# Normalizing products that read in order and write with a step of four columns, and two last stores issued whole

## The chip, the core and the metric

The kernel runs on one core of one Trainium2 chip. The metric is the device time of one execution in microseconds (us). Five engines work at the same time, each through its own queue of instructions: TensorE (PE) multiplies matrices, VectorE (DVE) and ScalarE (ACT) do elementwise work, GpSimd (POOL) does casts and issues some DMAs, and SyncE (SP) issues most DMAs. ACT's queue can issue DMAs too. SBUF is the on-chip memory, 128 partitions with one row each; PSUM is the smaller memory that PE writes.

## The reference

Sliding-window attention of 8 batches, 8 heads, 576 positions and 64 channels per head, followed by a two-layer network with a tanh GELU:

```python
B, H, S, D = q.shape                      # 8, 8, 576, 64
scores = (1 / np.sqrt(D)) * np.matmul(q, k.transpose(0, 1, 3, 2))
mask = np.abs(pos[:, None] - pos[None, :]) <= 32
scores = np.where(mask, scores, -1e9)
attn = softmax(scores)                    # over the last axis
x = np.matmul(attn, v).transpose(0, 2, 1, 3).reshape(B * S, H * D)   # 4608 tokens x 512
h = x @ w_in                              # w_in 512 x 2048
g = 0.5 * h * (1 + np.tanh(c * (h + 0.044715 * h ** 3)))
out = g @ w_out                           # w_out 2048 x 512, float32
```

## The kernel before

**Two streams of work on one PE.** The network runs over 9 tiles of 512 tokens (t = 0 to 8). While tile t is multiplied by w_out, the attention of batch b = t + 1 is computed in between: each loop step i issues one product of the network, and the tables PLAN_0, PLAN_1, PLAN_2, PLAN_L and PLAN say after which i a piece of attention is issued (s is a score, m a mask, g or v the sums and weighted values, x the normalizing product). So the order on each engine is written out by hand, and each engine runs its own list in order. Batches 0 and the start of the network are written out one by one ahead of the loop.

**Attention in groups.** A batch has five groups. Groups 0 to 3 are pairs of heads, 64 channels of two heads on the 128 partitions, with the first 480 tokens of the batch (512 in batch 0). Group 4 holds the last 96 tokens (64 in batch 0) of all four pairs. The function score (line 489) multiplies keys and queries on PE; line 502 takes the exponential on ACT; mask (line 511) multiplies by the band on DVE; sum_up (line 516) sums over the keys on PE, and times (line 526) multiplies by the values on PE; invert (lines 553 and 554) takes the logarithm and the exponential of its negative on ACT, which gives one over the sum, in the SBUF tile lt.

**The normalizing product.** The function spread (lines 564 and 571) multiplies the weighted values, which lie in PSUM as float32 (tiles ps_o, ps_od, mm), by lt, float32 in SBUF, on DVE, and writes float16 into xT, the input of the network. Queries are stored four ways interleaved: in PSUM and in lt the columns stand as (j p), j = 0 to 3 outside and p inside, where the token is 4 p + j. In xT the columns stand in the order of the tokens, (p j). So one side of the product has to be walked with a step. In this kernel the two operands are: `x[:, 0:n].rearrange("d (j p) -> d p j", j=4)` takes an element from each of the four rows j in turn, 120 float32 elements (480 bytes) apart in a group of 480, 128 (512 bytes) in batch 0 and 24 or 16 in group 4; the write runs through xT column by column. xT is a ring of 1,536 columns; where a batch crosses its end, line 564 is issued twice, with shorter pieces (192 and 288, or 384 and 96 elements).

**Who uses xT.** ffn_in (line 602) multiplies four chunks of w_in by the four pairs' rows of xT, chunk dc needing pair dc. For the next tile the first three columns n are begun with chunks 0 to 2 (dc = 0, 1, 2 of one column, then of the next) at the end of the loop over i; chunk 3 follows at the head of the next tile. Later tiles compute part of this product with seven half-size products in place of eight (in_product, line 658), for which DVE forms differences of blocks of xT (line 643) and of w_in (in_w, line 632). In w_in16 the columns that belong together are four apart, and in_w reads them through this view:

```python
w_cols = w_in16.rearrange("k d (i p j) -> k d i j p", i=4, j=4)
A11, A12, A21, A22 = (w_cols[:, d:d + 2, c + i, j:j + 2, :] for c in (0, 2) for d in (0, 2))
```

so that line 632 reads float16 elements in SBUF with a step of four columns (8 bytes), runs of 128 elements, and writes float16 without a step.

**The second layer.** ffn_out (line 789) computes gelu(h) by w_out with seven products n = 0 to 6 in place of eight. DVE takes each result out of PSUM (lines 800 to 821: n = 3 is line 812, n = 5 is line 821) and ffn_last (line 830) the last one. Two PSUM banks take turns, and n = 5 adds onto the bank that line 812 has to read first. The masks of the next groups stand on DVE behind such lines.

**Loads of the early batches.** For batch 2 SP issues, in this order, the loads of keys (line 204), two transposing DMAs of queries and keys (lines 435 and 443), which wait for casts on DVE (lines 431 and 441), and then four loads of values (line 416); POOL casts these (line 357), and DVE copies them to the other half of the partitions (pair_v, lines 236 and 237) for times. All DMAs of one queue are issued in the order of its list.

**Stores.** The function store (line 753) splits its rows evenly over the engines named. In the last tile the third quarter (line 823) is stored by SP and ACT in halves of 64 rows, and line 834 stores the last two blocks of 128 rows by 256 columns (block x = 0, then x = 1), each as 64 rows on SP and 64 rows on ACT.

Of the kernel before, what the change touches and what calls it, by code (L numbers as in the profile page):

```python
# [12 lines left out]
ALU = mybir.AluOpType  # L13
# [23 lines left out]
def cut(b):  # L37
    return 120 if b else 128
# [50 lines left out]
def kernel(  # L89
# [9 lines left out]
    nc = tc.nc  # L99
# [3 lines left out]
    NPAIR = H // 2  # L103
# [39 lines left out]
    xT = big.tile([128, NPAIR, RING], FP16, name="xT")  # L143
# [395 lines left out]
    def weigh(b, g, pair=None):  # L539
        pe = groups.pop((b, g))  # L540
        o, d = out_of(pair)
        sum_up(b, g, d, pe)
        times(b, g, o, pe)
        return o, d

    def size(b, g):
        return 4 * cut(b) if g < 4 else 4 * NPAIR * (144 - cut(b))
# [9 lines left out]
    def spread(b, g, o, lt):  # L557
        n = size(b, g)
        if g < 4:
            pos, done, w = b * S % RING, 0, cut(b)  # L560
            by_row = [x[:, 0:n].rearrange("d (j p) -> d p j", j=4) for x in (o, lt)]
            while done < w:
                e = min(w - done, (RING - pos) // 4)
                nc.vector.tensor_tensor(  # L564
                    xT[:, g, pos:pos + 4 * e].rearrange("d (p j) -> d p j", j=4),
                    *(x[:, done:done + e, :] for x in by_row), op=ALU.mult)
                done, pos = done + e, (pos + 4 * e) % RING
        else:
            pos = (b * S + 4 * cut(b)) % RING
            assert pos + n // NPAIR <= RING  # L570
            nc.vector.tensor_tensor(
                xT[:, :, pos:pos + n // NPAIR].rearrange("d r (p j) -> d r p j", j=4),
                *(x[:, 0:n].rearrange("d (r j p) -> d r p j", r=NPAIR, j=4) for x in (o, lt)), op=ALU.mult)


    gTs = {}
# [170 lines left out]
    def store(t, t4, yo, cols=slice(0, 512), *engs):  # L747

        r0 = t * 512 + t4 * 128
        engs = engs or (nc.gpsimd,)  # L750
        rows = 128 // len(engs)
        for i, eng in enumerate(engs):
            eng.dma_start(out[r0 + i * rows:r0 + i * rows + rows, cols], yo[i * rows:i * rows + rows, cols])  # L753
# [71 lines left out]
    def ffn_last(t):  # L825
        py = pys[0].rearrange("p (b c) -> p b c", b=2)
        yo, right = wino["yo"], slice(256, 512)
        for x in range(2):
            part = pys["apart"][:, 0:256] if x and t == NT - 1 else py[:, x, :]
            nc.vector.tensor_tensor(yo[:, x, right], part, yo[:, x, right], op=ALU.add)  # L830
            if t < NT - 1:
                store(t, x, yo[:, x, :])
            else:
                store(t, x, yo[:, x, :], right, nc.sync, nc.scalar)


    cast_open(0)
# [50 lines left out]
    def finish(g, o):  # L888
        times(0, g, o, groups.pop((0, g)))
        spread(0, g, o, lts[g])  # L890
# [80 lines left out]
    for t in range(NT):  # L971
# [58 lines left out]
        for i in range(113 if t else 65):  # L1030
# [9 lines left out]
            for act in plan.get(i, "").split():  # L1040
                kind, at = act[0], int(act[act.index("@") + 1:]) if "@" in act else None
                g = int(act[1:].split("@")[0])
# [16 lines left out]
                elif kind in "np":  # L1059
# [7 lines left out]
                    if kind == "n":  # L1067
                        n = size(1, g)
# [21 lines left out]
                elif kind in "ab":  # L1090
                    if b < B - 1:
                        if kind + str(g) == "a0":
                            cast_open(b + 1)
                        turn_query(b + 1, g) if kind == "a" else turn_keys(b + 1, (g,))
                elif kind == "g":
                    two = []
                    for gg, pair in ((g, at), (g + 1, None)) if g >= 0 else ((2, None), (g, at)):
                        two.append((gg, *group(gg), *out_of(pair), groups.pop(group(gg))))
                    for gg, bb, g1, o, d, pe in two:
                        sum_up(bb, g1, d, pe)  # L1100
                    for gg, bb, g1, o, d, pe in two:
                        times(bb, g1, o, pe)
                    for gg, bb, g1, o, d, pe in two:
                        ods[gg] = (o, invert(bb, g1, d))
                    if g < 0:
                        load_vt(b + 1)
                    if t > 1 and g == 2:
                        load_table(gelu_set)
                elif kind == "v":
                    bb, gg = group(g)  # L1110
                    o, d = weigh(bb, gg, at)
                    ods[g] = (o, invert(bb, gg, d))
                    if t and g < 0 and b + 1 < B:
                        load_vt(b + 1)
                    if t > 1 and g == (3 if att else -1):
                        load_table(gelu_set)
                else:
                    spread(*group(g), *ods[g])
# [16 lines left out]
        if t == 0:  # L1135
            wino_rest(B12)
            load_table(gelu_set)
        else:
            ffn_last(t)
# [31 lines left out]
```

## Time and profile before

| | |
|---|---|
| median of 3 runs | 296.28 us (295.19 to 296.58) |
| the profiled execution | 295.1 us, of which the span from its first to its last instruction is 293.2 us |
| busy: PE, weight loads, DVE, ACT, POOL | 283.9, 196.6, 237.7, 196.8, 66.5 us |
| TensorE clock granted | 0.998 |
| normalizing products | line 564 40 times, line 571 8 times |

A line of groups gives the line of the kernel, the engine, the operation, what it writes and reads, the shape and the count, then the busy time in us, the mean of one in ns, and the idle time of the engine just before them with what ended it. A line of the timeline gives the start in us, the time that the merged run of instructions took, the engine, line, operation and count, and in brackets idle time ahead of it and what ended it. Matmuls overlap: 128x512 ones that follow each other without a wait start 0.216 us apart, though each is shown as 0.38 us long. A queue's own instructions carry a q (SPq, ACTq): for a DMA that is the time that the issue takes, not the transfer.

### The profile page before, as it was taken

The numbers are of one execution on the slowest core, as the hardware profiler recorded it, in microseconds if no ns is written. First come the engines' busy times: TensorE is split into PE (matmuls) and PEld (weight loads), VectorE is DVE, ScalarE is ACT, GpSimd is POOL, SyncE is SP. The second block draws the span as 40 slices with busy tenths as digits, with TensorE's granted clock in tenths as the row PEclk, the third lists the DMA queues.
The fourth block names the chain that finished last, engine by engine and source line by source line (L and its number), as shares of the span: only waits on it lengthen the run. The fifth ranks groups of instructions, "written<-read, shape, count | busy, mean of one in ns | idle before, by whom it ended". The sixth has DMA issues, their size and how long they took to land.

```text
span 293.2 us, 7364 instructions
## 1 busy us (share of the span) xinstructions
PE 283.9 (97%) x2993; PEld 196.6 (67%) x2993; DVE 237.7 (81%) x499; ACT 196.8 (67%) x323; POOL 66.5 (23%) x109
## 2 busy tenths in 40 slices
PE   8889999999999999999999999999999999999994
PEld 3535544557775688668856876688667877887783
DVE  4775377999997988899998899889988987875682
ACT  5865867779477876588558945894679576904800
POOL 4435325102327071105025003500300020011000
PEclk9999999999999999999999999999999999999999
DMA  7999997989999999859998989698810030003014
GB/s 226 274 373 401 353 311 191 252 168 191 263 211 189 242 237 203 241 133 225 131 249 218 182 118 209 179 180 104 244 18 2 2 143 3 0 2 144 0 38 107
DMA packets 112481, 51.00 MB, mean 174 GB/s; under 512 B 96768, under 2 KB 108544, under 8 KB 112192
## 3 DMA queue, kind: packets, MB, share of 16 engines
q1 hardware_dynamic: 89584, 38.81, 59.1%
q0 software_dynamic: 21840, 10.82, 21.3%
q10 hardware_dynamic: 1024, 0.92, 1.1%
q8 instruction: 23, 0.38, 0.6%
q14 instruction: 10, 0.08, 0.1%
HBM read 36.70 MB, written 9.44 MB: 157 GB/s over the span
## 4 chain that ended last, share of the span: by engine, by line
PE 79%; DVE 8%; DMA 6%; SPq 3%; issue 2%; ACT 1%; POOL 1%; ACTq 0%; DVEq 0%
PE mm L789 29%; PE ph L602 15%; PE mm L602 12%; PE pu L658 7%; PE ps_s L489 3%; PE mm L761 2%; DMA wst<-in_moe_w_in_dram 2%; PE py L761 2%; DVE xT L564 2%; SPq L282 2%; DMA vr<-in_v_dram 2%; DVE t L733 2%; DMA qr<-in_q_dram 1%; PE ps_d L516 1%; PE ps_od L516 1%
## 5 line engine op out<-in xcount | busy, mean ns | idle before, releaser
L602 PEld LDWEIGHTS <-w_in 128*128 128x128 f16 x448 | 50.1, 113 | 40.2 <-issue 1.2
L602 PE MATMUL ph<-xT,w_in 128*128 128x512 f16 x240 | 60.2, 379 | 0.3 <-POOL w_in L261 0.3
L602 PE MATMUL mm<-xT,w_in 128*128 128x512 f16 x208 | 53.9, 379 | 0.6 <-DVE xT L564 0.5
L789 PEld LDWEIGHTS <-s 128*128 128x128 f16 x512 | 49.4, 98 | 6.2
L789 PE MATMUL mm<-t,s 128*128 128x256 f16 x376 | 44.9, 273 | 0.0
L789 PEld LDWEIGHTS <-gT 128*128 128x128 f16 x384 | 36.1, 98 | 7.3 <-issue 1.0
L502 ACT ACTIVATE pe<-ps_s 128x960 f16<-128x960 f32 (+1 forms) x31 | 29.5, 975 | 13.7 <-PE ps_s L489 13.6
L753 POOL DMA_DIRECT2D out_dram<-y x28 | 15.2, 548 | 98.9 <-DVE y L821 93.6
L789 PE MATMUL mm<-w_out,gT 128*128 128x256 f16 x256 | 32.6, 273 | 0.0
L610 ACT ACTIVATE gT<-mm 128x512 f16<-128x512 f32 x28 | 16.5, 599 | 22.8 <-PE mm L602 22.5
L743 DVE TENSOR_TENSOR s<-gT 128x512 f16<-128x512 f16 x64 | 26.6, 421 | 5.3 <-ACT gT L610 2.3
L610 ACT ACTIVATE gT<-ph 128x512 f16<-128x512 f32 x38 | 20.9, 607 | 6.8 <-PE ph L602 6.8
L114 ACT ACT_TABLE_LOAD x18 | 23.1, 1283 | 2.2 <-issue 1.9
L554 ACT ACTIVATE lt<-lt 128x480 f32<-128x480 f32 (+3 forms) x36 | 21.1, 585 | 1.2
L511 DVE TENSOR_TENSOR pe<-pe,band 128x960 f16<-128x960 f16 x28 | 18.1, 664 | 0.7 <-ACT pe L502 0.5
L564 DVE TENSOR_TENSOR xT<-ps_od,lt 128x480 f16<-128x480 f32 (+4 forms) x18 | 14.8, 848 | 3.4 <-ACT lt L554 2.2
L526 PEld LDWEIGHTS <-V 128*64 128x64 f16 x520 | 12.6, 112 | 6.5 <-DVE V L237 2.3
L564 DVE TENSOR_TENSOR xT<-ps_o,lt 128x480 f16<-128x480 f32 (+5 forms) x20 | 15.2, 783 | 1.9 <-PE ps_o L526 1.7
L706 ACT ACTIVATE gT<-ph 128x512 f16<-128x512 f32 x22 | 13.2, 601 | 4.8 <-PE ph L602 4.7
L789 PE MATMUL mm<-t,gT 128*128 128x256 f16 x128 | 16.2, 273 | 0.2
L743 DVE TENSOR_TENSOR s<-s,gT 128x512 f16<-128x512 f16 x32 | 14.5, 452 | 1.1
L553 ACT ACTIVATE lt<-ps_od 128x480 f32<-128x480 f32 (+2 forms) x13 | 7.1, 546 | 11.5 <-PE ps_od L526 6.7
(153 smaller groups left out, 484.7 us busy)
## 6 DMA issues: line engine op xcount, KB each, us to landing
kr<-in_k_dram SPq DMA_DIRECT2D x31, 256.0 KB, 8.2
out_dram<-y POOLq DMA_DIRECT2D x28, 256.0 KB, 3.5
qr<-in_q_dram SPq DMA_DIRECT2D x6, 1024.0 KB, 6.1
wst<-in_moe_w_in_dram SPq DMA_DIRECT2D x8, 512.0 KB, 7.8
vr<-in_v_dram SPq DMA_DIRECT2D x12, 256.0 KB, 5.9
wst<-in_moe_w_out_dram SPq DMA_DIRECT2D x2, 1024.0 KB, 10.5
wst<-in_moe_w_out_dram SPq DMA_DIRECT2D x4, 512.0 KB, 7.2
V<-in_v_dram POOLq DMA_DIRECT2D x16, 128.0 KB, 8.7
```

Of the source, the lines that this page charges most:

```text
L114: nc.scalar.add_instruction(mybir.InstLoadActFuncSet(name=nc.get_next_instruction_name(), act_func_set_id=which, ins=[], outs=[]))
L502: nc.scalar.activation(pe, ps[:, :, 0:w], AF.Exp, scale=SCALE)
L511: nc.vector.tensor_tensor(pe, pe, m.rearrange("k (o j) p -> k o j p", o=1).broadcast_to(list(pe.shape)), op=ALU.mult)
L554: nc.scalar.activation(lt[:, 0:n], lt[:, 0:n], AF.Exp, scale=-1.0)
L564: nc.vector.tensor_tensor(xT[:, g, pos:pos + 4 * e].rearrange("d (p j) -> d p j", j=4), *(x[:, done:done + e, :] for x in by_row), op=ALU. ...
L602: nc.tensor.matmul(ph, w_cols[:, dc, fc // 4, fc % 4, :], xT[:, dc, t * 512 % RING:t * 512 % RING + 512], start=(dc == 0), stop=(dc == 3))
L610: nc.scalar.activation(gTs[t][:, fc, :], phs[fc], AF.Gelu_apprx_tanh)
L658: nc.tensor.matmul(ps[:, 256 * h:256 * h + 256], lhs[:, d, h, :], rhs[:, d, :], start=(n in (0, 2, 4) and h == d == 0), stop=(h == d == 1) ...
L706: nc.scalar.activation(gTs[t][:, fc, :], phs[fc], AF.Gelu_apprx_tanh)
L743: nc.vector.tensor_tensor(dst, x, y, op=op)
L753: eng.dma_start(out[r0 + i * rows:r0 + i * rows + rows, cols], yo[i * rows:i * rows + rows, cols])
L789: nc.tensor.matmul(pys["apart"][:, 0:256] if apart else py[:, blk, :], lhsT, wino[w][:, f, :], start=(new and i % (8 if one else 16) == 0) ...
```

## The change

In spread the two operands are now read as they lie (four runs of 120, 128, 96, 48, 72 or 24 elements, or 24 and 16 in group 4), and the write into xT goes along with them, with a step of four columns (8 bytes) from one element to the next. The number of instructions, the elements of each and all waits stay; on DVE line 564 has the form 128x4x120 where it had 128x480. In ffn_last each of the last two blocks is stored whole, 128 rows by 256 columns: block 0 from ACT's queue, block 1 from SP's. SP and ACT issue one DMA each where they issued two; nothing else changes its place on any engine.

```diff
@@ spread
-            by_row = [x[:, 0:n].rearrange("d (j p) -> d p j", j=4) for x in (o, lt)]
+            by_row = [x[:, 0:n].rearrange("d (j p) -> d j p", j=4) for x in (o, lt)]
...
                 nc.vector.tensor_tensor(
-                    xT[:, g, pos:pos + 4 * e].rearrange("d (p j) -> d p j", j=4),
-                    *(x[:, done:done + e, :] for x in by_row), op=ALU.mult)
+                    xT[:, g, pos:pos + 4 * e].rearrange("d (p j) -> d j p", j=4),
+                    *(x[:, :, done:done + e] for x in by_row), op=ALU.mult)
...
             nc.vector.tensor_tensor(
-                xT[:, :, pos:pos + n // NPAIR].rearrange("d r (p j) -> d r p j", j=4),
-                *(x[:, 0:n].rearrange("d (r j p) -> d r p j", r=NPAIR, j=4) for x in (o, lt)), op=ALU.mult)
+                xT[:, :, pos:pos + n // NPAIR].rearrange("d r (p j) -> d r j p", j=4),
+                *(x[:, 0:n].rearrange("d (r j p) -> d r j p", r=NPAIR, j=4) for x in (o, lt)), op=ALU.mult)
@@ ffn_last
-                store(t, x, yo[:, x, :], right, nc.sync, nc.scalar)
+                store(t, x, yo[:, x, :], right, (nc.scalar, nc.sync)[x])
```

## The prediction

> **What bounds the kernel now.** I read the page first, then the chain that ended last, then the groups by form, then the timeline at the places where PE starts late.
>
> ```profile
> PE 283.9 (97%) x2993; PEld 196.6 (67%) x2993; DVE 237.7 (81%) x499; ACT 196.8 (67%) x323; POOL 66.5 (23%) x109
> ...
> PE 79%; DVE 8%; DMA 6%; SPq 3%; issue 2%; ACT 1%; POOL 1%; ACTq 0%; DVEq 0%
> ```
>
> PE is the bound. A shorter DVE instruction is worth only what PE waits for DVE, so the sum has to be made at single places. What the products cost today, and what comparable DVE work costs, by form:
>
> ```profile
> L564 DVE TENSOR_TENSOR xT<-ps_od,lt 128x480 f16<-128x480 f32 x12 | 11.6, 990 | 3.0 <-ACT lt L554 1.8 <-PE ps_od L526 1.2
> ...
> L830 DVE TENSOR_TENSOR y<-mm,y 128x256 f32<-128x256 f32 x15 | 5.7, 419 | 0.9 <-PE mm L789 0.9
> ...
> L821 DVE TENSOR_TENSOR y<-mm,y 128x512 f32<-128x512 f32 x8 | 5.5, 690 | 2.9 <-PE mm L789 2.9
> ...
> L632 DVE TENSOR_TENSOR wcA<-w_in 128x512 f16<-128x512 f16 x2 | 1.4, 696 | 0.0
> ...
> L564 DVE TENSOR_TENSOR xT<-ps_o,lt 128x96 f16<-128x96 f32 x3 | 0.9, 304 | 0.0
> ```
>
> Lines 821 and 830 have the same operands as the product (one in PSUM, one in SBUF, float32) without a step: (690 - 419) / 256 = 1.06 ns per element and 148 ns fixed. The product takes (990 - 304) / 384 = 1.79 ns per element and 132 ns fixed. So reading with a step of 480 bytes costs 0.73 ns more per element.
>
> **Cost of the products after.** Reading in order takes the 0.73 ns away. What the write with a step of 8 bytes adds, no row shows: nothing in the trace writes single elements with a step. The nearest row is line 632, which reads two float16 operands in SBUF with this same step of 8 bytes and takes 696 ns for 512 elements, (696 - 148) / 512 = 1.07 ns per element: no more than a walk without a step. The bounds: at least the unstepped rate, 148 + 480 x 1.06 = 657 ns; at most twice the penalty that the read pays now, 990 + 480 x 0.73 = 1340 ns; between them lies 990, a write that costs what the reads cost. Below 657 nothing is in sight, since the same-shaped rows without any step are not faster. I take 657, by the row with the same step. Saved: 333 ns on each of 20 products of 480, about 360 on the 4 of 512 (1047 to 691), 257 on 11 of 384 (812 to 555), 198 on 4 of 288, 130 on 4 of 192, little on the rest, some 12 of DVE's 237.7 us.
>
> [...]
>
> **Where PE waits for these products.**
>
> ```profile
> 51.80 3.69 DVE L564 TENSOR_TENSOR xT<-ps_od,lt 128x480 f16<-128x480 f32 x4 [1.20 <-PE ps_od L526]
> ...
> 53.24 0.88 PE L602 MATMUL mm<-xT,w_in 128*128 128x512 f16 x2
> ...
> 54.64 0.38 PE L602 MATMUL mm<-xT,w_in 128*128 128x512 f16 x1 [0.51 <-DVE xT L564]
> ...
> 80.25 0.33 PE L516 MATMUL ps_od<-pet,ones 128*64 128x384 f16 x2
> ...
> 80.87 0.42 PE L526 MATMUL ps_o<-pe,V 128*64 128x96 f16 x14 [0.28 <-DVE xT L564]
> ```
>
> First place: the first chunks of tile 1 need pairs 0, 1 and 2 in turn. At the pace of 0.216 us the third matmul would start at 53.24 + 0.43 = 53.67; it starts at 54.64, 0.97 late. The products start 0.92 apart; after, 0.59 apart, so the third ends at 51.80 + 1.18 + 0.66 = 53.64. Gain 0.95.
>
> Second place: two sums of 0.16 us start at 80.25, so the next could start near 80.5; with the base cost of a switch it is 0.35 late, behind four products (two of 384, two of 96: 0.6 us saved). Gain 0.35, if DVE also keeps up with PE's earlier arrival (below).
>
> ```profile
> 171.57 0.70 DVE L812 TENSOR_TENSOR y<-mm,y 128x512 f32<-128x512 f32 x1
> ...
> 172.33 1.03 PE L789 MATMUL mm<-t,gT 128*128 128x256 f16 x8
> ...
> 173.04 0.65 DVE L511 TENSOR_TENSOR pe<-pe,band 128x960 f16<-128x960 f16 x1
> ...
> 173.74 0.39 PE L516 MATMUL ps_d<-pe,ones 128*64 128x480 f16 x2
> ```
>
> Third: line 812 frees the bank that n = 5 adds onto; PE could start at 172.02 (nine matmuls of 0.109 from 171.04), so it is 0.31 late, and the mask behind makes it 0.25 late again at 173.74. Ahead of line 812 stand two split products of 1.06 us each (192 and 288 elements), which lose 0.33 each; 0.66 covers the 0.56. The same place in the next two tiles (202.63 and 232.77, unsplit products) is 0.17 and 0.19 late. Gain 0.9 in all.
>
> The four products of batch 0 (14.3 to 22.1 us) gain nothing: PE at 21.27 waits for POOL's cast of w_in, and that for a DMA that lands at 20.55; the casts hide them. From 84 to 165 and after 235 PE shows no late start beyond 0.2 us that DVE ends: PE's matmuls hide those products.
>
> **What is next late.** The gain at 54 must survive the chain that runs through DVE, SP and the loads of batch 2's values:
>
> ```profile
> 68.94 5.27 DMA vr<-in_v_dram
> 74.21 0.05 issue
> 74.27 0.86 POOL V L357
> 75.12 0.02 issue
> 75.14 0.80 DVE V L236
> 75.94 0.01 issue
> 75.95 0.42 DVE V L237
> ```
>
> PE needs these values from 76.3 us, with no slack. SP issues the loads behind two transposes (63.59 and 64.95) that wait for DVE's casts, and those stand on DVE behind the four products at 51.80, without idle time between. So the casts come 4 x 0.33 = 1.3 us earlier, and SP's transposes and loads with them, into a stretch in which the DMA engines idle (41 to 55 KB per us at 63 to 65 us against 200 to 250 around it). I take it that the values keep up with the 0.95.
>
> **The last stores.** The final product ends at 289.01 + 0.42 = 289.43. SP then still issues block 0's half, and starts block 1's at 289.81; ACT's starts at 290.11 and lands last, 2.0 us on. After, each queue has one issue left: ACT's queue is free at 289.4 and SP's at 289.15, so both start near 289.45. The 128 KB stores at 282.7 land in 1.8 us, the second 0.48 behind the first; two at once would land near 291.3 and 291.8 in place of 292.1. Bounds: 0.6 gained, if both land in 2 us; 0.3 lost, if 256 KB at once queue behind the third quarter's halves. I take 0.25 gained. Nobody waits for them but the end.
>
> **Sum.** 0.95 + 0.35 + 0.9 + 0.25 = 2.45 us. The profiled execution took 295.1 us, 1.9 of it outside the span of 293.2, so it becomes 292.7. It lies 1.2 below the median, at the low end of the three runs; the difference goes onto the median: 296.28 - 2.45 = 293.8. I write 294.0, since the 0.35 needs DVE to keep its lead.
>
> **Rivals.**
> - *Given back at the values.* If the transposes or loads take no earlier slot (SP's own issue of line 435 ends at 62.0 whatever DVE does), PE waits at 76.3 for what it saved at 54. Left: 0.35 + 0.9 + 0.25 = 1.5; 294.8 us. For it: SP's list is in order and the DMA share there is 0.98. Against: the idle DMA stretch.
> - *The step moves, and with it the price.* The write pays what the reads paid; the products stay at 990 ns, and only the stores change: 296.0 us. For it: one stepped stream might cost as much as two. Against: line 632.
> - *Slower: the write is dearer than the reads were.* It decides as soon as a product of 480 takes over 990 ns. At the upper bound, 1340 ns, the third product at 51.8 ends 3 x 0.35 = 1.05 later, and PE with it; at 80.87 DVE is 4 x 0.35 + 0.7 = 2.1 later, less PE's 1.05; line 812 comes 0.7 later in three tiles (2.1) and, with 0.2 of idle time before it, 0.5 later in the two tiles before (1.0). Together 5.2, less 0.25 at the stores: 301.2 us. [...]
>
> **How the numbers follow.** Forecast 0.56, given back 0.14, price moved 0.14, slower 0.16. A difference under 0.5%, 1.48 us, is about what a measurement of this kernel can't tell from none. Of the forecast 0.88 lies beyond that, of the second case half: faster 0.56. Same 0.27: the third case, and what is left of the first two. Slower 0.17. The range goes from 293.0 (all gains, and 0.6 at the stores) to 297.2 (the third case with the runs' spread of 0.6 and a slightly dearer write); it leaves out the dear write. The likeliest case alone spans 293.0 to 294.9.
>
> **What would show it.** Right: line 564 at 480 elements near 657 ns; the matmul of line 602 that starts at 54.64 follows its neighbours at 0.216 us; no late start before line 526 near 80; line 812 ends before PE needs its bank; the values of batch 2 are on DVE about 1 us earlier; two issues fewer at the end. Wrong: a product of 480 at 900 ns or more sinks the sum at once; PE's late start moving from 54 to 76 is the first rival; last landings later than 2.7 us after the last product turn the stores' sign.

## The result and the profile after

The changed kernel is slower: 297.29 us (median) against 295.81 for the kernel before beside it, ratio 1.0062 with a 95% interval of 1.0032 to 1.0091. The ratio is taken over the runs and amounts to about 1.8 us; the two medians lie 1.5 us apart. The forecast was 2.3 us faster. The profiled execution took 296.96 us with a span of 295.3 us (295.10 and 293.2 before).

The busy times of the profile page and the products by form, after:

```profile
PE 284.8 (96%) x2993; PEld 197.1 (67%) x2993; DVE 245.0 (83%) x499; ACT 196.8 (67%) x323; POOL 66.7 (23%) x109
```

```profile
L564 DVE TENSOR_TENSOR xT<-ps_od,lt 128x480 f16<-128x480 f32 x12 | 14.4, 1247 | 2.8 <-ACT lt L554 1.8 <-PE ps_od L526 1.0
...
L564 DVE TENSOR_TENSOR xT<-ps_o,lt 128x96 f16<-128x96 f32 x3 | 1.2, 417 | 0.0
```

A product of 480 takes 1247 ns in place of 990 (657 were forecast), one of 96 takes 417 in place of 304: (1247 - 417) / 384 = 2.16 ns per element, where the stepped read took 1.79. DVE is busy 7.3 us longer. The timeline at the first and the second place of the prediction, and at the bank of line 812:

```profile
51.93 4.46 DVE L564 TENSOR_TENSOR xT<-ps_od,lt 128x480 f16<-128x480 f32 x4 [1.04 <-PE ps_od L526]
...
54.30 0.38 PE L602 MATMUL mm<-xT,w_in 128*128 128x512 f16 x1 [0.54 <-DVE xT L564]
...
55.36 0.38 PE L602 MATMUL mm<-xT,w_in 128*128 128x512 f16 x1 [0.69 <-DVE xT L564]
...
81.91 0.42 PE L526 MATMUL ps_o<-pe,V 128*64 128x96 f16 x14 [0.60 <-DVE xT L564]
...
174.05 1.03 PE L789 MATMUL mm<-t,gT 128*128 128x256 f16 x8 [0.31 <-DVE y L812]
```

PE now waits for the second product and for the third (before, visibly for the third alone), and it waits longer before line 526 at 81.91 and behind line 812 at 174.05. Since PE issues the same 2993 matmuls in the same order, each can be set against its own start before. The delay of PE grew at these matmuls:

| matmul (start before) | waits for | delay added, us |
|---|---|---|
| up to 53.2 us | | 0.13 |
| line 602, 53.75 and 54.64 | the second and third product | 0.59 |
| line 526, 80.87 | the bank that line 564 reads | 0.31 |
| line 526, 136.08 | the bank that line 571 reads | 0.12 |
| line 602, 146.97 | the last products of its tile | 0.28 |
| line 658, 151.91, 182.35, 212.47 | the bank that line 693 copies out on DVE | 0.11, 0.22, 0.21 |
| line 789, 172.33 (and 173.74) | the bank that line 812 reads | 0.17 (-0.18) |
| line 789, 202.63 and 232.77 | the same in the next two tiles | 0.34, 0.30 |
| sum at the last matmul | | 2.61 |

The span grew by 2.10 only. From the end of the last product (289.43 before, 292.04 after) to the end of the span it was 3.72 us and is 3.22: the stores give 0.50 back.

### The profile page after: what moved, and what is told of

Its sections match the earlier page's. It is cut to its first block, busy times and chain, and to the rows that moved or that the text cites. A ratio compares the mean times of both kernels' runs of the same rounds, so it can differ in the third digit from the quotient of the medians.

```text
span 295.3 us, 7360 instructions
## 1 busy us (share of the span) xinstructions
PE 284.8 (96%) x2993; PEld 197.1 (67%) x2993; DVE 245.0 (83%) x499; ACT 196.8 (67%) x323; POOL 66.7 (23%) x109
## 4 chain that ended last, share of the span: by engine, by line
PE 46%; DMA 22%; DVE 16%; SPq 10%; issue 2%; ACT 1%; POOL 1%; ACTq 0%; DVEq 0%
PE mm L789 19%; PE ph L602 8%; PE mm L602 8%; DMA qt<-in_q_dram 6%; DMA kr<-in_k_dram 5%; PE pu L658 5%; SPq L204 5%; DMA vr<-in_v_dram 4%; DVE xT L564 3%; DMA tr<-in_q_dram 3%; DMA wst<-in_moe_w_out_dram 3%; SPq L282 1%; DMA qr<-in_q_dram 1%; DVE qt L423 1%; DVE k L441 1%
## 5 line engine op out<-in xcount | busy, mean ns | idle before, releaser
L743 DVE TENSOR_TENSOR s<-gT 128x512 f16<-128x512 f16 x64 | 27.2, 429 | 4.8 <-ACT gT L702 2.1
L564 DVE TENSOR_TENSOR xT<-ps_od,lt 128x480 f16<-128x480 f32 (+4 forms) x18 | 18.1, 1071 | 3.2 <-ACT lt L554 2.2
L564 DVE TENSOR_TENSOR xT<-ps_o,lt 128x480 f16<-128x480 f32 (+5 forms) x20 | 18.9, 993 | 1.5 <-PE ps_o L526 1.4
L743 DVE TENSOR_TENSOR s<-s,gT 128x512 f16<-128x512 f16 x32 | 13.9, 434 | 1.1
```

Of the source, the lines that this page charges most:

```text
L564: nc.vector.tensor_tensor(xT[:, g, pos:pos + 4 * e].rearrange("d (p j) -> d j p", j=4), *(x[:, :, done:done + e] for x in by_row), op=ALU. ...
L743: nc.vector.tensor_tensor(dst, x, y, op=op)
```

## The experiments

Each timed kernel ran beside the kernel before on the same chip; ratios are to that. The code cuts are shortened, with ... where lines are left out.

**The price of a step by itself.** A kernel that only repeats single instructions, 480 elements per partition, one operand stepped at a time. In the cut, order is a walk in order, hops a read with a step of 480 bytes, and rows with stepped a read in order with a stepped write.

```diff
...
+mul(order(halves("psumread")), hops(o), order(sb))       # only PSUM read with a step of 480 bytes
+mul(order(halves("sbufread")), order(o), hops(sb))       # only SBUF
+mul(stepped(halves("write_four")), rows(o), rows(sb))    # only the write, float16, step 4
+mul(stepped(floats("float_four")), rows(o), rows(sb))    # only the write, float32, step 4
...
```

> A kernel of its own that leaves the whole computation out: it repeats single instructions on 480 elements per partition, four times each, with one operand walked with a step at a time, and is read by the mean duration of each form. In order a product of PSUM and SBUF float32 into float16 should take 655 to 660 ns, both reads stepped 980 to 990 (the form of before), the write of float16 with a step of four 1250 (the form of after). Theory A, a write that leaves its 8-byte granule after one element is what costs, whatever its width: float16 with a step of two (4 bytes, two elements per granule) stays within 100 ns of 660; steps of 8 and 16 cost 1250 or more; float32 with a step of two (8 bytes) costs about 1250 too. Theory B, the half word is what costs (a 2-byte write that has no neighbour to fill the word): float16 with a step of two costs about 1250 as well, and float32 with a step of two or four stays near 660 to 990. For the reads: if PSUM's step is free the product with only PSUM stepped takes 660 and the one with only SBUF stepped 980; if it is the other way round, the reverse. ScalarE: a stepped read of PSUM free means about 560 ns as in order.

The groups by form, VectorE and then ScalarE; the second number behind the bar is the mean in ns:

```profile
L56 DVE TENSOR_TENSOR write_eight<-o,sb 128x480 f16<-128x480 f32 x4 | 9.1, 2286 | 0.1
...
L56 DVE TENSOR_TENSOR write_four<-o,sb 128x480 f16<-128x480 f32 x4 | 4.9, 1214 | 0.1
L56 DVE TENSOR_TENSOR float_four<-o,sb 128x480 f32<-128x480 f32 x4 | 4.0, 1000 | 0.1
L56 DVE TENSOR_TENSOR bothread<-o,sb 128x480 f16<-128x480 f32 x4 | 3.9, 966 | 0.1
L56 DVE TENSOR_TENSOR sbufread<-o,sb 128x480 f16<-128x480 f32 x4 | 3.9, 963 | 0.1
...
L56 DVE TENSOR_TENSOR write_two<-o,sb 128x480 f16<-128x480 f32 x4 | 2.8, 690 | 0.1
...
L56 DVE TENSOR_TENSOR inorder<-o,sb 128x480 f16<-128x480 f32 x4 | 2.6, 658 | 0.8 <-PE o L34 0.7
L56 DVE TENSOR_TENSOR psumread<-o,sb 128x480 f16<-128x480 f32 x4 | 2.6, 658 | 0.1
L56 DVE TENSOR_TENSOR float_two<-o,sb 128x480 f32<-128x480 f32 x4 | 2.6, 656 | 0.1
...
L76 DVE CAST copy_sbufread<-sb 128x480 f16<-128x480 f32 x4 | 2.3, 574 | 0.1
```

```profile
L76 ACT COPY act_sbufread<-sb 128x480 f32<-128x480 f32 x4 | 4.0, 1010 | 0.1
...
L76 ACT COPY act_order<-sb 128x480 f32<-128x480 f32 x4 | 2.4, 592 | 0.1
L76 ACT COPY act_order_psum<-o 128x480 f32<-128x480 f32 x4 | 2.2, 558 | 67.6 <-DVE copy_psumread L76 67.5
L76 ACT COPY act_psumread<-o 128x480 f32<-128x480 f32 x4 | 2.2, 556 | 0.1
```

The forms of before (966) and after (1214) are there without the rest of the kernel, so nothing of the surroundings is needed to explain them. Of the two stepped reads of the product SBUF's costs everything (963) and PSUM's nothing (658, as much as all in order). ScalarE's copies behave alike: 1010 with a step in SBUF against 592 in order, 556 against 558 in PSUM. But VectorE's copy of one operand from SBUF with the same step takes 574, so the 963 is the price of the product, not of every read. A copy from PSUM alone into float16 with a step of four takes 1215, so the price of the write needs no operand in SBUF. The write is where both theories fall: half words with a step of two are cheap (690, against B), and float32 at the very step of 8 bytes is free (656, against A), while float16 at 8 bytes takes 1214 and at 16 bytes 2286. From there the price of lone half words no longer grows: 2236 at 32 bytes (write_sixteen), 2286 at 240 (write_far).

**Products alone, stores alone.**

```diff
-                store(t, x, yo[:, x, :], right, (nc.scalar, nc.sync)[x])     # prods_alone: after, with this undone
+                store(t, x, yo[:, x, :], right, nc.sync, nc.scalar)
-                store(t, x, yo[:, x, :], right, nc.sync, nc.scalar)          # stores_alone: before, with this alone
+                store(t, x, yo[:, x, :], right, (nc.scalar, nc.sync)[x])
```

> The new products with the old stores. Theory 1 (the written step costs DVE 260 ns per product of 480, PE pays 2.6 us of it, the stores give 0.5 back): 2.3 us slower than before, ratio 1.007 to 1.009, slower than with both parts. Rival (the stores are what costs, the products are hidden by PE): the same time as before, ratio 0.999 to 1.002.

> The old products with the new stores. Theory 1: 0.3 to 0.5 us faster than before, ratio 0.998 to 0.999, with the span ending about 3.3 us after the last product in place of 3.7. Rival (the stores are what costs): 1.5 us slower, ratio 1.005.

The products alone give 298.33 us, ratio 1.0066 (1.0025 to 1.0107); the stores alone 294.81, ratio 0.9961 (0.9928 to 0.9994). Both ratios lie below their expected ranges, with intervals that reach them. The change is a loss and a gain of opposite sign. The stores' share is clearest at the end: 3.76 us from the last product to the end of the span with the old stores (prods_alone), 3.20 with the new ones (stores_alone); the last landing comes 2.71 and 2.17 us after that product. Of the profiled execution of prods_alone only this end is used: its instructions up to the stores are those of after, yet at 145 us a cast of keys (line 441) waited 1.4 us for its load, and PE lost 1.73 us near 147 where it lost 0.28 in after. So the moment at which a load of keys lands differs from one execution to the next.

**What is the unit of the price?** Single instructions again, now with steps between the ones above.

```diff
...
+for name, step in (("half_two", 2), ("half_three", 3), ("half_four", 4), ("half_six", 6), ("half_eight", 8)):
+    mul(sparse(name, step), flat(o), flat(sb))            # float16, one element every `step`
+for name, step in (("pair_four", 4), ("pair_eight", 8), ("pair_sixteen", 16)):
+    mul(sparse(name, step, run=2), flat(o, 2), flat(sb, 2))
...
```

> Single instructions again, 480 elements, without the computation. Theory C, a line of 16 bytes is the unit: a line that gets only half words costs 4.5 ns of writing, a line that gets whole words or is read 1.8 ns, and an instruction takes the larger of that and 660 ns. Then float16 with a step of two, three, four, six, eight takes 690, about 950 (180 lines), 1214, about 1750 (360 lines), 2290; pairs of float16 (a whole word) with a step of four stay at 660, of eight and sixteen 1000; float32 with a step of two 656, of three about 780, of four and eight 1000; float32 reads in SBUF with a step of two 660, of four and eight 960. Theory D, the cost goes by the element (an element that is not next to the last one pays): float16 with steps of three and six cost like four or eight, about 1214 and 2290, without values between; pairs pay half of single elements at the same step, over 1000 ns.

```profile
L56 DVE TENSOR_TENSOR half_six<-o,sb 128x480 f16<-128x480 f32 x4 | 7.1, 1764 | 0.1
...
L56 DVE TENSOR_TENSOR half_three<-o,sb 128x480 f16<-128x480 f32 x4 | 3.8, 957 | 0.1
...
L56 DVE TENSOR_TENSOR float_three<-o,sb 128x480 f32<-128x480 f32 x4 | 3.2, 790 | 0.1
...
L56 DVE TENSOR_TENSOR read_two<-o,far 128x480 f16<-128x480 f32 x4 | 2.6, 657 | 0.1
L56 DVE TENSOR_TENSOR pair_eight<-o,sb 128x480 f16<-128x480 f32 x4 | 2.6, 655 | 0.1
```

Theory C holds for writes. Its 16 bytes are the step at which the price of a write stops growing (2286 there and 2236 at 32 for half words, 995 and 1016 for float32), and the values between, 957 for 180 lines of 16 bytes and 1764 for 360, come out within 15 ns of what it gave, and theory D has no place for them. A line of 16 bytes written in lone half words costs (2286 - 1214) / 240 = 4.5 ns, one written in whole words (1000 - 790) / 120 = 1.75 ns. On top of either stands a fixed part that the expectation left out in words, though its figures need it: 1214 - 240 x 4.47 = 141 ns and 1000 - 480 x 1.75 = 160 ns. Two of its figures missed clearly. Pairs with a step of eight or sixteen visit 240 lines, not 480, which is 160 + 240 x 1.75 = 580 ns, less than the 655 of a product in order (float_order); they take 655, not 1000. Pairs with a step of four took 707 where 660 stood. Reads of SBUF ran only with steps at which each line gives two elements (657) or one (988 at 16 bytes, 1005 at 32), without a value between; that they too are priced by the line fits, but is not shown.

**The step where it is free.** If PSUM may be read with a step for nothing, as the 658 ns of VectorE and the 556 of ScalarE say, lt can be put into the order of the tokens by the logarithm, which reads PSUM on ScalarE, and the product keeps only its free step. (In the cut r is 1 in groups 0 to 3 and 4 in group 4; the product of group 4 and the logarithms of batch 0 are changed in the same way.)

```diff
-        nc.scalar.activation(lt[:, 0:n], d[:, 0:n], AF.Ln)
+        nc.scalar.activation(tokens(lt, n, r), rows(d, n, r), AF.Ln)   # d read as (r j p) -> r p j, lt written in order
-            by_row = [x[:, 0:n].rearrange("d (j p) -> d p j", j=4) for x in (o, lt)]
+            by_row = [rows(o, n)[:, 0], tokens(lt, n)[:, 0]]           # o stepped, lt and xT in order
...
```

> The old products with one operand changed: the logarithm on ScalarE reads the sums in PSUM with the step and writes lt in the order of the tokens, so that the product reads only PSUM with a step and writes xT in order. From the single instructions (only PSUM stepped 658 ns, ScalarE reading PSUM stepped 556 against 558 in order): a product of 480 takes 660 ns in place of 990, the logarithm stays at 550. Theory 1 (the prediction's places are right and only the price of the step was wrong): the third matmul at 54.64 comes 0.95 us earlier, 0.35 more is gained at 81 and 0.8 at the three banks, 2.1 us in all, ratio 0.992 to 0.994. Rival (what is gained at 54 is given back at 76 where the values of batch 2 arrive): 1.2 us, ratio 0.996. Second rival (a stepped read on ScalarE costs 350 ns more in place, as its stepped reads of SBUF did): the products start later by as much and nothing is gained.

292.96 us against 295.62, ratio 0.9896 (0.9859 to 0.9932): a larger gain than theory 1 gave, with an interval that reaches its range. By form, then the timeline at the first place, then the waits from 168 to 174 us (engine, what it waited for, us in total, times, longest):

```profile
L564 DVE TENSOR_TENSOR xT<-ps_od,lt 128x480 f16<-128x480 f32 x12 | 7.6, 653 | 3.1 <-ACT lt L554 1.8 <-PE ps_od L526 1.3
```

```profile
51.73 2.35 DVE L564 TENSOR_TENSOR xT<-ps_od,lt 128x480 f16<-128x480 f32 x4 [1.31 <-PE ps_od L526]
...
53.18 0.81 PE L602 MATMUL mm<-xT,w_in 128*128 128x512 f16 x3
```

```profile
DVE k L441 <- DMA kr<-in_k_dram: 1.4, 1, 1.4
...
PE ps_d L516 <- DVE pe L511: 1.0, 1, 1.0
```

The product takes 653 ns, the logarithm 556 (555 before), which rules out the second rival, and the three matmuls of line 602 follow each other without a wait. In the trace PE gains 0.96 at 54, 0.47 at 81 and 0.31, 0.17 and 0.19 at the three banks, further 0.13 at 76 and 0.18 at 152, which the prediction didn't name, and loses 1.0 at 173.74, where the cast of the next keys stands on VectorE ahead of a mask and its load has not landed. The span is 1.5 us shorter, the median 2.7; the profiled execution (293.56 us) lies 0.6 above the median of its runs, and that of before (295.10) 0.5 below 295.62.

**With the stores, and with the keys moved.** lt_in_order_stores adds the new stores. keys_later also moves one step of the plan:

```diff
-        63: "s3@0 s4@1", 66: "b0 b1", 70: "m3", 74: "m4", 80: "b2 b3"
+        63: "s3@0 s4@1", 70: "m3", 74: "m4 b0 b1", 80: "b2 b3"
```

> The same with the two last blocks stored whole. Theory 1: a further 0.5 us, 2.6 us in all, ratio 0.990 to 0.993. Rival (given back at the values): 1.7 us, ratio 0.994 to 0.996.

> The kernel of lt_in_order_stores with one step of the plan moved: in tiles 4 and 5 the first two casts of the next keys stand on VectorE behind the masks of groups 3 and 4, not ahead of them. In both runs before, the cast in tile 4 waited 1.4 to 1.6 us for its keys to land and held the mask, for which PE then waited 1.05 to 1.2 us. Theory (the gain of the earlier banks is given back at this load, 1.0 us of it): the wait of PE at the sums of tile 4 goes, 1.0 us less than lt_in_order_stores and 3.6 us less than before, ratio 0.986 to 0.989. Rival (the load holds whatever comes next on VectorE, line 815 and then the products, as long): the wait moves to a place at most 3 us later, and the time stays that of lt_in_order_stores, ratio 0.990 to 0.992.

lt_in_order_stores: 293.69 us, ratio 0.9917 (0.9881 to 0.9954); its interval overlaps that of lt_in_order, so the runs don't show the further gain, though the trace does (3.20 us from the last product to the end, against 3.75). Its profiled execution, and that of stores_alone, got a load of values near 14 us about 2 us later than the others, ahead of all that differs, so only what follows is compared. keys_later: 291.94 us against 295.93, ratio 0.9874 (0.9837 to 0.9911), the fastest here:

```profile
170.03 0.65 DVE L511 TENSOR_TENSOR pe<-pe,band 128x960 f16<-128x960 f16 x1
...
171.72 0.37 PE L516 MATMUL ps_d<-pe,ones 128*64 128x480 f16 x2
```

The mask is done 1.0 us before PE needs it, and no wait for the keys shows up to 174 us. So the microsecond that lt_in_order gave back was the load in front of the mask. In time, keys_later and lt_in_order_stores can't be told apart surely, since their intervals overlap.

**One batch alone.** The stepped write in groups 0 to 3 of batch 1, all else as before.

```diff
+            step = "d j p" if b == 1 else "d p j"
...
```

> The stepped write in batch 1 alone (groups 0 to 3, the four products at 52 us), all else as before. Theory 1: those four take 1250 ns; PE's third matmul at 54.64 comes 0.7 to 0.8 us later than its neighbours ahead of it did, and at 81 PE waits 0.1 to 0.3 us more, and nothing else moves; 0.8 us slower. Rival (the cost is spread over PE's later waits alone): no change near 54 us.

```profile
55.39 0.38 PE L602 MATMUL mm<-xT,w_in 128*128 128x512 f16 x1 [0.69 <-DVE xT L565]
```

PE loses 0.60 us at this place (0.42 and 0.18 at the second and third product), as with the whole change (0.59) and a little less than the 0.7 to 0.8 expected. The span at the end is 0.69 longer, of which 0.16 was there ahead of these products. The further 0.1 to 0.3 at 81 us didn't come, so that what after loses there belongs to the four products just ahead of it. The single time, 295.78 us, says nothing at this size.

## Why the prediction was wrong

One more row of before bears on the first point: line 643, a difference of float16 operands in SBUF, 512 elements, without a step.

```profile
L643 DVE TENSOR_TENSOR xw<-xT 128x512 f16<-128x512 f16 x8 | 3.4, 419 | 0.0
```

- *The price of the write* ("I take 657, by the row with the same step") is the step that failed: a read stood for a write. A write of lone half words with a step of 8 bytes takes 1214 ns alone and 1247 in the kernel, where 657 stood, so each product of 480 became 257 ns dearer instead of 333 cheaper. The row had the right step and the wrong direction; float32 reads of SBUF with that step do take 657 ns (read_two). Nor was line 632 free of its own step. It takes 696 ns, was set against float32 rows, and the row above, of the same shape and type without a step, takes 419. The measured 1247 lies inside the bounds of 657 to 1340, but the upper one was twice the read's penalty, a figure that no row gave for a write: that it held is luck.
- *The price of the read* was right in size (990 to 653 without it, 333 ns forecast) and put on both operands; SBUF's alone pays it (963 ns, against 658 with only PSUM stepped).
- *The places and their terms* held. Given products of 653 ns, lt_in_order gains 0.96, 0.47 and 0.31 + 0.17 + 0.19 where 0.95, 0.35 and 0.9 stood (0.31 + 0.25 + 0.17 + 0.19); the 0.25 of the mask turned into a loss of 1.0 at a load that the sum had not named.
- *Given back at the values* did not happen in lt_in_order: the last values land at 72.84 us in place of 74.21, 1.37 earlier (1.3 was argued), and PE has no wait there. In keys_later 0.5 us came back at that place: its first values land late, at 70.99 (70.04 before), and its last at 73.33, so this rival stays possible from one execution to the next.
- *The slower rival* is the mechanism that came, 2.1 us of span in place of its 4.95. Its price was 350 ns per product and 257 were measured; and a product's tail lies beside the next one: the four at 52 us start 1.06 us apart in place of 0.90, so 0.16 of the 0.257 counts for each product ahead of the last. Its 1.05 at 54 became 0.59, its 1.05 at 81 became 0.31, its 2.1 at three banks 0.63. The two tiles before lost nothing at their banks and 0.39 at 147 and 152 instead, and 0.55 came at 136, 182 and 212, which it did not name.
- *The stores*: 0.25 was taken, 0.50 came. Both issue 0.03 us after the last product, and the last landing is 2.17 us behind it in place of 2.70; "the sign" turned at 2.7, which was not reached.
- *The chances*: 0.17 for slower was too little for a price that no row showed. Reads stood for writes, and the range was cut below the upper bound that the same text worked out.

## What to carry to other kernels

Price a step by the direction, the memory, the width and the instruction: a free stepped read of PSUM (658 ns, as in order) said nothing of a stepped write of half words (1214), and read_two (657) nothing of it at the same 8 bytes. If data has to be reordered, try it where the step is read from PSUM, with SBUF's reads and writes in order (a product of 653 ns in place of 990); here that turned a change of +0.6% into one of -1.0%, and -1.3% with the new stores and the plan mended, though the intervals of these two overlap. After a gain look for what stands in the same queue ahead of the next work: a load's cast in front of a mask took back 1.0 us.

## What the runs showed of the hardware

- A stepped read of PSUM (480 elements of float32, 480 bytes from one to the next) cost nothing on VectorE (658 ns against 658) and ScalarE (556 against 558).
- VectorE's stepped writes to SBUF fit a price by visits to lines of 16 bytes: about 1.75 ns for whole words (790 ns for 360 lines, 1000 for 480) and 4.5 ns for lone half words (957 for 180, 1214 for 240, 1764 for 360, 2286 for 480), and no price where that comes to less than a product in order (655 ns for 240 lines of pairs). The product's stepped reads of SBUF fit the 1.75 at the steps that ran (657 ns at 8 bytes, 988 at 16, 1005 at 32); the copy of one operand (574 ns with a step of 480 bytes) does not, and why was not tried.
- Single words 8 bytes apart in SBUF cost nothing (657 read, 656 written, 658 in order); half words written 8 bytes apart took 1214.
- Why a line of half words costs 2.5 times one of whole words (4.5 ns against 1.75) was not tried.
